# Attention units regrouped by batch in eight phases, mask factors copied instead of computed, and two banks for the first keys' results

## The chip, the cores and the metric

The kernel runs on one core of one Trainium2 chip. The metric is the device time of one execution in microseconds (us); lower is better. The kernel before takes 308.17 us, the median of three runs (307.17 to 308.41).

## The reference

Attention with a sliding window of 128 keys and a linear distance bias, followed by a two-layer MLP with the gate h * cos(h). There are 8 batches, 8 heads, 576 positions and 64 columns per head; the MLP sees 4608 tokens of 512 columns and has 2048 hidden columns.

```python
scores = scale * np.matmul(q, k.transpose(0, 1, 3, 2))
slopes = 2.0 ** (-8.0 * (np.arange(H, dtype=np.float32) + 1) / H)
bias = slopes[:, None, None] * (-np.abs(rel).astype(np.float32))[None, :, :]
mask = (rel >= 0) & (rel < window)
scores = np.where(mask, scores + bias[None], -1000000000.0)
scores = scores - np.max(scores, axis=-1, keepdims=True)
attn = np.exp(scores)
attn = attn / (np.sum(attn, axis=-1, keepdims=True) + 1e-09)
...
x = np.ascontiguousarray(attn_out.transpose(0, 2, 1, 3)).reshape(B * S, H * D)
h = x @ w_in
g = h * np.cos(h)
return (g @ w_out).astype(np.float32)
```

## The kernel before

**Units.** Attention is cut into 64 units, eight for each batch, named (batch, block, half): 128 queries by four heads, mostly. Batches 0 and 1 use blocks that begin at multiples of 128; their first and last units hold all eight heads (the last one 64 queries), and the others four. Batches 2 to 7 use *offset* units: blocks of 128 queries that begin 64 later, and the first 64 queries of the batch are computed along with the two units of block 0 ("first keys", lines 817 to 820). A unit goes through score matmuls on TensorE (PE) (L701, or L661 and L675 for offset units), an exponential on ScalarE (ACT) (L757, L735, L748), a multiplication with mask factors on VectorE (DVE) (L794, or L773, L775 and L780), context matmuls with the values (L841 and L843, L829 and L833, or L813 and L815; L819 for first keys), and a division by the row sums on DVE (L885 and L887; L896 and L898 for first keys). The result is transposed into xT, either by DMA (L962, L965, issued by SyncE, SP) or by PE with a copy behind it (L920, L939).

**The MLP** works on nine chunks of 512 tokens. The first layer of a chunk is 64 matmuls of 512 columns (L978), with cos on ACT (L983) and the gate on DVE (L987); the second layer is 64 matmuls as well (L1031), sixteen for each of four tiles of 128 tokens, with a copy (L1038, L1039) and a store (L1043).

**Phases.** The loop over chunks c (L1144) makes one phase each: the first layer of chunk c, then attention units that later chunks need, then the second layer of chunk c. Seven units of batch 0 run ahead of chunk 0. `QUOTA` has how many units a phase takes, `GROUPS` how they are cut; the units of one group share one block of score matmuls. A group of four is a *side* group, whose scores lie side by side in six banks (`home`, L629) and whose exponentials cover two units each. `SLOT` has the banks of other groups, `SIDE` those of the context results of a group of four, `SIDE_KEY` those of the first keys' results.

**The order** is a planner's. Every operation has an occupancy, a latency, a priority (smaller goes first) and the tiles it reads and writes (`op`); `schedule` (L95) lists them greedily by these costs, and each engine then runs its own list in order, with semaphores for what crosses engines. So a change in groups or costs moves instructions on all engines. Scores have priority 2, context 1, the first layer 5 and the second layer 6: on PE the layers fill what attention leaves.

**Loads.** POOL's queue issues the loads of weights, queries, keys and values. For offset batches SP issues the transposes of queries and keys (L447, L450), and three copies of the values shifted by 64 rows (L424, L426, L428) into the space of the first query or key rows (named qrows or krows); the context matmuls of offset units read values and shifted copy. Of a phase's units, the first four (two in phase 0) are always transposed by DMA; the others by DMA if their tokens belong to a chunk after the next, otherwise by PE (L1097 to L1108).

**Mask factors.** Units of batches 0 and 1 multiply with a table `EM`, the exponential of the biases. Offset units use three tables of their own, `own_em` (in the buffer qfirst), `out_em` (in the buffer bias) and `key_em` (in the buffer kfirst), that `band_factors` (L504) makes during phase 0: distances by POOL, window by DVE, 24 exponentials by ACT.

Of the kernel before, what the change touches and what calls it, by code (L numbers as in the profile page):

```python
# [6 lines left out]
ALU = mybir.AluOpType  # L7
ACTF = mybir.ActivationFunctionType
# [279 lines left out]
def bass_alibi_sliding__then__act_gcu_kernel(  # L288
# [8 lines left out]
    with ExitStack() as ctx:  # L297
# [37 lines left out]

        bdif, boff = sb("bdif", [128, 384], F32), sb("boff", [128, 384], F32)


        own_em = qF["q"][:, :, :].rearrange("p a b -> p (a b)").bitcast(BF16).rearrange(
# [11 lines left out]

        GROUPS = [[2] * 4, [4, 3, 1]] + [[4, 4]] * 4 + [[4, 3, 2]]
        SLOT = [4, 6, 2]

        SIDE, SIDE_KEY = [2, 5, 4, 7], [3, 3, 6, 6]

        FIRST, FIRST_PV = [0, 1, 2, 0, 1, 0, 1], [0, 0, 2, 2, 3, 2, 3]
        QUOTA = [8, 8, 8, 8, 8, 8, 9]
        BIASED = [(0, 0, 0)] + [(0, qb, hh) for qb in range(1, 4) for hh in range(2)][:5]
# [144 lines left out]
        def band_factors():  # L504
            op("pool", lambda e: e.iota(bdif[:, 64:192], pattern=[[192, 2], [-1, 64]], base=-192,
                                        channel_multiplier=1,
                                        allow_small_or_imprecise_dtypes=True),
               w=["bdif"], occ=400, lat=480)
            op("pool", lambda e: e.iota(bdif[:, 192:256], pattern=[[-1, 64]], base=-64,
                                        channel_multiplier=1,  # L510
                                        allow_small_or_imprecise_dtypes=True),
               w=["bdif"], occ=300, lat=380)
            op("pool", lambda e: e.iota(bdif[:, 256:384], pattern=[[-1, 128]], base=-64,
                                        channel_multiplier=1,
                                        allow_small_or_imprecise_dtypes=True),
               w=["bdif"], occ=400, lat=480)
            op("dve", lambda e: e.memset(bdif[:, 0:64], -1.0e6), w=["bdif"], occ=100, pri=7)
            op("dve", lambda e: e.memset(bdif[0:64, 192:256], -1.0e6), w=["bdif"], occ=100, pri=7)
            for edge, test in [(-127.0, ALU.is_lt), (0.0, ALU.is_gt)]:
                op("dve", lambda e, edge=edge, test=test: e.tensor_scalar(  # L520
                    boff[:, :], bdif[:, :], edge, -1.0e6, test, ALU.mult),
                   r=["bdif"], w=["boff"], occ=300, lat=380, pri=7)
                op("dve", lambda e: e.tensor_tensor(bdif[:, :], bdif[:, :], boff[:, :], ALU.add),
                   r=["boff"], w=["bdif"], occ=450, lat=530, pri=7)
            for h in range(H):
                g = band_head(h)
                for o, lo, hi, w in [
                        (own_em[:, g, :], 256, 384, [("qF", "q")]),
                        (out_em[0][:, g, :], 64, 192, [("BT", i) for i in range(0, H, 2)]),
                        (key_em[:, g, :], 192, 256, [("qF", "k")])]:  # L530
                    op("act", lambda e, o=o, lo=lo, hi=hi, s=slopes[h]: e.activation(
                        o, bdif[:, lo:hi], ACTF.Exp, scale=s),
                       r=["bdif"], w=w + ["bem"], occ=180 + (hi - lo) * 5 // 7,
                       lat=280 + (hi - lo) * 5 // 7, table=2, pri=7)
            op("dve", lambda e: e.memset(out_em[1][:, :, 0:64], 0.0),
               w=[("BT", i) for i in range(1, H, 2)] + ["bem"], occ=300, pri=7)
            op("dve", lambda e: e.tensor_copy(out_em[1][:, :, 64:128],
                                              out_em[0][:, :, 64:128]),
               w=["bem"], occ=330, lat=410, pri=7)
# [509 lines left out]
        def attention(us, phase):  # L1049
# [4 lines left out]
            for many in sizes:  # L1054
# [89 lines left out]
        for c in range(NCH):  # L1144
# [64 lines left out]
```

## Time and profile before

| | |
|---|---|
| median of three runs | 308.17 us (307.17, 308.17, 308.41) |
| the profiled execution's own time | 307.02 us |
| its span in the trace | 305.2 us |
| PE, DVE, ACT, POOL busy | 97%, 66%, 65%, 32% of the span |
| granted PE clock | 1.00 |
| first layer of chunk 1, first matmul | at 53.92 us |
| second layer of chunks 1 to 6, first matmul | at 67.73, 100.68, 132.58, 164.95, 195.82 and 227.20 us |
| last matmul of the second layer | ends near 302.8 us |

Times in the trace count from the start of the span. Matmuls are pipelined and their ends are modelled, so the distance of two starts tells more than a length; a few per cent of the matmul records are missing. A line number is that of the kernel before.

### The profile page before, as it was taken

To read this page: it belongs to the slowest core of one execution; us is meant where nothing else is said; L and a number is where in the kernel's file an instruction comes from. 1 tells how busy PE (TensorE), PEld (TensorE's weight loads), DVE (VectorE), ACT (ScalarE), POOL (GpSimd) and SP (SyncE) were. 2 spreads that over 40 slices of the span, in tenths; PEclk is the share of its full clock that TensorE was granted. 3 is DMA by queue.
4 is the path that set the end of the run, shared out by engine and by line. 5 is a ranking of instruction groups with operands and counts; after the bars stand their busy time and mean duration, and the time that the engine had idled before them with its cause. 6 is when DMAs were issued, how large, how long until landed. Compare 5 with 4: busy or idle time off the path is not lost.

```text
span 305.2 us, 7209 instructions
## 1 busy us (share of the span) xinstructions
PE 296.6 (97%) x2900; PEld 156.8 (51%) x2945; DVE 200.3 (66%) x482; ACT 198.0 (65%) x292; POOL 96.9 (32%) x124
## 2 busy tenths in 40 slices
PE   8999999999999999999999999999999999999996
PEld 6585455445554455445544554455445554444444
DVE  6687867585778568848686768766984778844000
ACT  6887889985378817882687467846777368854211
POOL 8997200555057304470357006620500000000000
PEclk9999999999999999999999999999999999999999
DMA  8999999999499936999799939997996320001122
GB/s 146 178 207 206 207 163 172 165 212 207 81 133 184 229 70 95 130 181 248 94 171 190 212 65 144 152 167 192 150 109 198 95 74 5 2 0 69 71 76 96
DMA packets 151408, 42.32 MB, mean 139 GB/s; under 512 B 138832, under 2 KB 145616, under 8 KB 151376
## 3 DMA queue, kind: packets, MB, share of 16 engines
q0 software_dynamic: 100416, 18.10, 79.8%
q1 hardware_dynamic: 50688, 23.51, 36.4%
q8 instruction: 23, 0.38, 0.5%
q10 hardware_dynamic: 272, 0.26, 0.3%
q14 instruction: 9, 0.07, 0.1%
HBM read 36.70 MB, written 9.44 MB: 151 GB/s over the span
## 4 chain that ended last, share of the span: by engine, by line
PE 86%; DMA 7%; POOL 4%; issue 2%; ACT 0%; POOLq 0%; ACTq 0%
PE ps L1031 40%; PE ps L978 36%; DMA w_outb<-in_moe_w_out_dram 7%; PE ps L661 2%; PE ps L813 2%; PE ps L815 2%; POOL vp L412 1%; PE ps L675 1%; POOL w_inb L459 1%; PE ps L701 1%; POOL qrows L405 1%; POOL krows L405 1%; PE ps L819 0%; PE ps L939 0%; POOL w_outb L466 0%
## 5 line engine op out<-in xcount | busy, mean ns | idle before, releaser
L1031 PE MATMUL ps<-w_outb,gT 128*128 128x512 bf16 (+2 forms) x564 | 130.3, 373 | 2.9 <-issue 2.1
L978 PE MATMUL ps<-xT,w_inb 128*128 128x512 bf16 x529 | 119.7, 379 | 0.8 <-issue 0.2
L983 ACT ACTIVATE cos<-ps,halfpi 128x512 f32<-128x512 f32 x136 | 89.7, 689 | 23.5 <-PE ps L978 17.7
L987 DVE TENSOR_TENSOR gT<-ps,cos 128x512 bf16<-128x512 f32 x136 | 90.2, 688 | 20.8 <-ACT cos L983 16.0
L1031 PEld LDWEIGHTS ps<-w_outb,gT 128*128 128x128 bf16 x592 | 53.8, 98 | 56.6 <-DMA w_outb<-in_moe_w_out_dram 1.1
L978 PEld LDWEIGHTS ps<-xT,w_inb 128*128 128x128 bf16 x544 | 51.5, 98 | 59.9 <-DVE gT L987 1.0
L412 POOL DMA_DIRECT2D vp<-in_v_dram x40 | 33.7, 868 | 92.3 <-DMA xT<-xnat 71.3
L1038 ACT ACTIVATE ob<-ps 128x512 f32<-128x512 f32 (+2 forms) x24 | 13.9, 579 | 46.3 <-PE ps L1031 30.3
L735 ACT ACTIVATE p<-ps 128x768 bf16<-128x768 f32 x40 | 31.3, 809 | 13.9 <-PE ps L675 13.3
L438 POOL DMA_DIRECT2D qnat<-in_q_dram x30 | 25.3, 877 | 17.5 <-DMA qt<-qnat 17.5
L438 POOL DMA_DIRECT2D knat<-in_k_dram x30 | 25.3, 873 | 10.3 <-DMA kt<-knat 7.6
L1039 DVE COPY ob<-ps 128x512 f32<-128x512 f32 x13 | 9.0, 692 | 27.2 <-PE ps L1031 27.2
L887 DVE TENSOR_TENSOR xnat<-ps,rec 128x256 bf16<-128x256 f32 x60 | 24.9, 419 | 0.6
L773 DVE TENSOR_TENSOR p<-p,qfirst 128x512 bf16<-128x512 bf16 x48 | 19.0, 414 | 8.1 <-ACT p L735 4.9
L757 ACT ACTIVATE p<-ps 128x1024 bf16<-128x1024 f32 x16 | 15.8, 1027 | 7.8 <-PE ps L675 4.0
L775 DVE TENSOR_TENSOR p<-p,bias 128x512 bf16<-128x512 bf16 x48 | 19.0, 411 | 0.2
L813 PEld LDWEIGHTS ps<-vp,p 128*128 128x128 bf16 x192 | 14.8, 97 | 7.2 <-issue 2.7
L813 PE MATMUL ps<-vp,p 128*128 128x65 bf16 x192 | 18.0, 193 | 0.1
L885 DVE RECIPROCAL rec<-ps 128x4 f32<-128x4 f32 x60 | 10.2, 176 | 8.3 <-PE ps L815 5.1
L661 PE MATMUL ps<-qt,kt 64*64 64x128 bf16 x384 | 10.2, 220 | 0.0
L661 PEld LDWEIGHTS ps<-qt,kt 64*64 64x64 bf16 x384 | 7.7, 108 | 4.9 <-issue 3.0
L748 ACT ACTIVATE p<-ps 128x768 bf16<-128x768 f32 x8 | 6.0, 810 | 5.8 <-PE ps L675 5.8
(105 smaller groups left out, 232.4 us busy)
## 6 DMA issues: line engine op xcount, KB each, us to landing
out_dram<-ob SPq DMA_DIRECT2D x35, 256.0 KB, 5.3
vp<-in_v_dram POOLq DMA_DIRECT2D x32, 128.0 KB, 6.4
qnat<-in_q_dram POOLq DMA_DIRECT2D x24, 128.0 KB
knat<-in_k_dram POOLq DMA_DIRECT2D x24, 128.0 KB, 6.9
w_outb<-in_moe_w_out_dram POOLq DMA_DIRECT2D x4, 512.0 KB, 21.9
w_inb<-in_moe_w_in_dram POOLq DMA_DIRECT2D x3, 512.0 KB, 11.5
qrows<-vp SPq DMA_DIRECT2D x3, 264.0 KB, 5.2
krows<-vp SPq DMA_DIRECT2D x3, 264.0 KB, 5.0
```

What stands on the lines that cost most here:

```text
L412: op("pool", [lambda e, t=t, rows=rows: e.dma_start(vp[b % 2][0:rows, t, :, 0:64], v[b, :, 128 * t:128 * t + rows, :].rearrange("h p d -> ...
L438: fns.append(lambda e, t=t, rows=rows: e.dma_start(nat[which][0:rows, t, :, :], src[b, :, 128 * t:128 * t + rows, :].rearrange("h p d -> p ...
L661: ins = e.matmul(flat[64 * half:64 * half + 64, c0:c0 + 128], kt[lo, j, pr, 64 * half:64 * half + 64], two, start=True, stop=True)
L735: op("act", lambda e, x=x, c0=c0: e.activation(p_all[:, i:i + 2, 384 * x:384 * x + 384], flat[:, c0:c0 + 768].rearrange("p (u f) -> p u f" ...
L773: op("dve", lambda e: e.tensor_tensor(p1, p1, own_em[:, gs, :], ALU.mult), r=[("P", i), "bem"], w=[("P", i)], occ=330, lat=420, pri=1)
L775: op("dve", lambda e: e.tensor_tensor(o, p2[:, :, None, :].broadcast_to([128, 4, 2, 64]), out_em[0 if qb else 1][:, gs, :].rearrange("p g ...
L813: e.matmul(o, P[i][:, c0:c0 + 128], V[:, qb, h, 0:65], start=True, stop=False)
L887: op("dve", lambda e: e.tensor_tensor(o, U[:, :, :, 0:64], rv[:, :, :, None].broadcast_to([128, 2, 2, 64]), ALU.mult), r=[("rec", n % 4)], ...
L978: op("pe", lambda e, kc=kc: e.matmul(ps[:, bank, :], w_in[:, kc, 128 * fc:128 * fc + 128], xT[:, kc, r0:r0 + CH], start=(kc == 0), stop=(k ...
L983: op("act", lambda e: e.activation(cosb[ci][:, :], ps[:, bank, :], ACTF.Sin, bias=halfpi[:, 0:1]), r=["halfpi"], w=[("B", bank), ("cos", c ...
L987: op("dve", lambda e: e.tensor_tensor(gT[gi][:, fc, :], ps[:, bank, :], cosb[ci][:, :], ALU.mult), r=[("cos", ci)], w=[("B", bank)] + [("g ...
L1031: op("pe", lambda e, t=t, fc=fc, bank=bank, j0=j0, j1=j1: e.matmul(ps[:, bank, 0:j1 - j0], gT[gi][:, fc, 128 * t:128 * t + 128], w_out[:, ...
```

## The change

1. The units of phase 0 are nine (one, then four pairs), so that all of batch 1 is done there; phases 1 to 6 take the eight units of one offset batch each, in two groups of four. The exchange that put the last unit of batch 1 among the second group of phase 1 is gone.
2. In a group of four, the results of the first keys go to bank 3 for half 0 and to bank 6 for half 1; before, it was by the place in the group.
3. `band_factors` copies `own_em` and `out_em` out of `EM` (six copies on ACT or DVE), fills the upper half of `key_em` with zeros and copies its lower half out of `own_em`. The three POOL operations, six DVE operations and 24 exponentials go, and the two buffers bdif and boff with them.
4. The loads of the next values and queries ask for one unit more than before (`>` for `>=`), which is the same phase as before, since a phase now ends one unit later.

```diff
-        bdif, boff = sb("bdif", [128, 384], F32), sb("boff", [128, 384], F32)
-        GROUPS = [[2] * 4, [4, 3, 1]] + [[4, 4]] * 4 + [[4, 3, 2]]
+        GROUPS = [[1] + [2] * 4] + [[4, 4]] * 6
-        SIDE, SIDE_KEY = [2, 5, 4, 7], [3, 3, 6, 6]
+        SIDE, SIDE_KEY = [2, 5, 4, 7], [3, 6]
-        QUOTA = [8, 8, 8, 8, 8, 8, 9]
+        QUOTA = [9, 8, 8, 8, 8, 8, 8]
...
         def band_factors():
-            op("pool", lambda e: e.iota(bdif[:, 64:192], pattern=[[192, 2], [-1, 64]], base=-192,
-                                        channel_multiplier=1,
-                                        allow_small_or_imprecise_dtypes=True),
-               w=["bdif"], occ=400, lat=480)
...
-            for h in range(H):
-                g = band_head(h)
-                for o, lo, hi, w in [
-                        (own_em[:, g, :], 256, 384, [("qF", "q")]),
-                        (out_em[0][:, g, :], 64, 192, [("BT", i) for i in range(0, H, 2)]),
-                        (key_em[:, g, :], 192, 256, [("qF", "k")])]:
-                    op("act", lambda e, o=o, lo=lo, hi=hi, s=slopes[h]: e.activation(
-                        o, bdif[:, lo:hi], ACTF.Exp, scale=s),
-                       r=["bdif"], w=w + ["bem"], occ=180 + (hi - lo) * 5 // 7,
-                       lat=280 + (hi - lo) * 5 // 7, table=2, pri=7)
+            for hh in range(2):
+                gs, ks = slice(4 * hh, 4 * hh + 4), slice(2 * hh, 2 * hh + 2)
+                for o, c0, n, w in [(own_em[:, gs, 0:64], 192, 64, [("qF", "q")]),
+                                    (own_em[:, gs, 64:128], 0, 64, [("qF", "q")]),
+                                    (out_em[0][:, gs, :], 64, 128,
+                                     [("BT", i) for i in range(0, H, 2)])]:
+                    o = o.rearrange("p (x k) f -> p x k f", x=2)
+                    i_ = EM[:, :, ks, c0:c0 + n]
+                    op(("act", "dve"),
+                       {"act": lambda e, o=o, i_=i_: e.activation(o, i_, ACTF.Copy),
+                        "dve": lambda e, o=o, i_=i_: e.tensor_copy(o, i_)},
+                       r=[("EM", 0), ("EM", 1), ("tr", "q", 1, 0)], w=w + ["bem"],
+                       occ={"act": 70 + 5 * n, "dve": 60 + 5 * n},
+                       lat={"act": 170 + 5 * n, "dve": 140 + 5 * n}, pri=7)
...
+            op("dve", lambda e: e.memset(key_em[0:64, :, :], 0.0), w=[("qF", "k"), "bem"],
+               occ=200, pri=7)
+            op("dve", lambda e: e.tensor_copy(key_em[64:128, :, :], own_em[64:128, :, 0:64]),
                w=["bem"], occ=330, lat=410, pri=7)
...
-                        kbank[u] = SIDE_KEY[n] if side else SLOT[n] + 1
+                        kbank[u] = SIDE_KEY[u[2]] if side else SLOT[n] + 1
...
         every = [u for b in range(B) for u in units(b)]
-        every.insert(19, every.pop(15))
...
-            while next_v < B and done >= 8 * (next_v - 1):
+            while next_v < B and done > 8 * (next_v - 1):
...
-            while next_t < B and done >= 8 * (next_t - 1):
+            while next_t < B and done > 8 * (next_t - 1):
```

Three places show what this does to the order on PE; the line numbers of the changed kernel are 11 smaller behind `band_factors`. The first is the start of phase 0, the first score block after chunk 0's first layer. Before (x is a count; 128x64 scores are those of batch 0's last unit, 128x128 those of batch 1):

```order
L978 MATMUL ps<-xT,w_inb 128x512 x7
L1031 MATMUL ps<-w_outb,gT0 128x512 x10
L701 MATMUL ps<-qt0,kt0 128x64 x16
L701 MATMUL ps<-qt1,kt1 128x128 x8
L1031 MATMUL ps<-w_outb,gT0 128x512 x14
```

And in the changed kernel:

```order
L967 MATMUL ps<-xT,w_inb 128x512 x7
L1020 MATMUL ps<-w_outb,gT0 128x512 x4
L690 MATMUL ps<-qt0,kt0 128x64 x16
L1020 MATMUL ps<-w_outb,gT0 128x512 x13
L690 MATMUL ps<-qt1,kt1 128x128 x16
```

The last unit of batch 0 has a block of its own, six second-layer matmuls earlier, and thirteen second-layer matmuls follow instead of fourteen. At the end of phase 0, the changed kernel leaves six of the 64 second-layer matmuls of chunk 0 for after chunk 1's first layer; before, none.

The second place is the end of phase 1. Before, behind the context matmuls of the second group (xtail1 is the last unit of batch 1):

```order
L1031 MATMUL ps<-w_outb,gT1 128x512 x2
L920 MATMUL ps<-ident,xtail1 128x64 x4
L1031 MATMUL ps<-w_outb,gT1 128x512
L939 MATMUL ps<-ident,xnat4 128x128 x2
L1031 MATMUL ps<-w_outb,gT1 128x512
L939 MATMUL ps<-ident,xnat5 128x128 x2
L661 MATMUL ps<-qt0,kt0 64x128 x8
L675 MATMUL ps<-qt0,kt0 64x64 x8
L978 MATMUL ps<-xT,w_inb 128x512 x9
```

And in the changed kernel:

```order
L928 MATMUL ps<-ident,xnat4 128x128 x2
L1020 MATMUL ps<-w_outb,gT1 128x512 x3
L928 MATMUL ps<-ident,xnat5 128x128 x2
L967 MATMUL ps<-xT,w_inb 128x512 x2
L802 MATMUL ps<-vp0,p 128x65
```

The transposes of the tail unit are gone (SP issues a DMA for it, behind the copies of batch 2's values), and so is the third score block, of a single unit. In the whole program PE has 40 transposes of results before and 32 after, and 18 and 17 blocks of scores in phases 0 to 6.

The third place is the first context block of phase 3, behind the last scores of its first group. Before (vp1 and krows are batch 3's values and shifted copy, vp0 and qrows batch 4's):

```order
L661 MATMUL ps<-qt0,kt0 64x128 x8
L675 MATMUL ps<-qt0,kt0 64x64 x8
L1031 MATMUL ps<-w_outb,gT1 128x512 x21
L813 MATMUL ps<-vp1,p 128x65
L815 MATMUL ps<-krows,p 128x65
```

And in the changed kernel:

```order
L650 MATMUL ps<-qt0,kt0 64x128 x8
L664 MATMUL ps<-qt0,kt0 64x64 x8
L1020 MATMUL ps<-w_outb,gT1 128x512 x21
L802 MATMUL ps<-vp0,p 128x65
L804 MATMUL ps<-qrows,p 128x65
```

The block stands 21 second-layer matmuls behind the scores in both, but it is batch 3's last unit before and batch 4's first unit after.

More of the change, by code (lines that the diff above doesn't have):

```diff
@@ L504, in band_factors @@
         def band_factors():
-            op("pool", lambda e: e.iota(bdif[:, 64:192], pattern=[[192, 2], [-1, 64]], base=-192,
-                                        channel_multiplier=1,
-                                        allow_small_or_imprecise_dtypes=True),
-               w=["bdif"], occ=400, lat=480)
[L509 to L524, printed above, removed]
@@ L538, in band_factors @@
                                               out_em[0][:, :, 64:128]),
+               w=["bem"], occ=330, lat=410, pri=7)
+            op("dve", lambda e: e.memset(key_em[0:64, :, :], 0.0), w=[("qF", "k"), "bem"],
+               occ=200, pri=7)
+            op("dve", lambda e: e.tensor_copy(key_em[64:128, :, :], own_em[64:128, :, 0:64]),
                w=["bem"], occ=330, lat=410, pri=7)
```

## The prediction, as it stands on record

> **What bounds the kernel now.** I read the page first, then TensorE's timeline, then the busy time by stages. The page gives the busy time of each engine and the shares of the chain that ended last.
>
> ```profile
> PE 296.6 (97%) x2900; PEld 156.8 (51%) x2945; DVE 200.3 (66%) x482; ACT 198.0 (65%) x292; POOL 96.9 (32%) x124
> ```
> ```profile
> PE 86%; DMA 7%; POOL 4%; issue 2%; ACT 0%; POOLq 0%; ACTq 0%
> ```
>
> TensorE ends the chain, but "97% busy" alone proves little, since a matmul's modelled length overlaps the next one's. The timeline settles it; its columns are start, length, engine, line, names and count. This is phase 1, in three pieces.
>
> ```profile
> 67.73 1.89 PE L1031 MATMUL ps<-w_outb,gT 128*128 128x512 bf16 x8
> 69.57 0.31 PE L661 MATMUL ps<-qt,kt 64*64 64x128 bf16 x8
> ...
> 70.62 4.48 PE L1031 MATMUL ps<-w_outb,gT 128*128 128x512 bf16 x20 [0.16 <-issue]
> 74.94 0.19 PE L813 MATMUL ps<-vp,p 128*128 128x65 bf16 x1
> ...
> 84.81 0.59 PE L1031 MATMUL ps<-w_outb,gT 128*128 128x512 bf16 x2
> 85.33 0.29 PE L920 MATMUL ps<-ident,xtail 64*128 64x64 bf16 x4
> 85.78 0.28 PE L939 MATMUL ps<-ident,xnat 128*128 128x128 bf16 x2 [0.16 <-issue]
> 85.89 0.38 PE L1031 MATMUL ps<-w_outb,gT 128*128 128x512 bf16 x1
> 86.11 0.28 PE L939 MATMUL ps<-ident,xnat 128*128 128x128 bf16 x2
> 86.31 0.31 PE L661 MATMUL ps<-qt,kt 64*64 64x128 bf16 x8
> ...
> 86.62 2.11 PE L978 MATMUL ps<-xT,w_inb 128*128 128x512 bf16 x9
> ```
>
> Twenty matmuls start within 4.48 - 0.38 = 4.10 us: 19 steps of 0.216 us. What follows a stream starts as its last step ends, so TensorE is not waiting here; each instruction taken from its queue shortens the run by its step. The Trainium skill's page "TensorE: Matmul & The Clock Gate", section "Back-to-back issue gap", gives about 131 ns as the sustained step of a 512-column matmul in a stream with weight loads. The trace disagrees, with 216 ns. By the page's figure some 40% of TensorE's time would be slack and the sum below would be zero.
>
> The stages agree that little waiting is left. In the table by stages, phase 2 and phase 3 (first column: from, to, length) do the same work and differ by 0.47 us; the timeline has a hole in the middle of a score block of phase 3, with no cause but "issue".
>
> ```profile
> 100.68:132.58 31.90, 31.37 (x325) 16.09 (x330) 23.07 (x57) 20.81 (x29) 9.45 (x12) 1.00 1.29 125
> 132.58:164.95 32.37, 31.62 (x326) 16.18 (x330) 23.07 (x57) 20.81 (x29) 15.60 (x19) 1.00 1.62 178
> ```
> ```profile
> 145.93 0.22 PE L675 MATMUL ps<-qt,kt 64*64 64x64 bf16 x3 [0.27 <-issue]
> ```
>
> **The change, step by step.** All sums stand against the profiled execution's own 307.02 us: 305.2 of span and 1.8 around it. That is 1.15 us under the median of 308.17; the prediction is put on the median's scale by adding that.
>
> *Transposes taken from TensorE: -0.54 us.* The tail unit of batch 1 moves from phase 1 to phase 0, where its tokens belong to a later chunk, so its four transposes (L920) become a DMA. From 85.33 to 85.89 stand, by the program's order, these four, one second-layer matmul (0.22, its record is missing) and one pair of transposes (0.11, from 85.78 to 85.89): 0.56 - 0.22 - 0.11 = 0.23. The two matmuls from 84.81 need 0.43 and the block starts 0.52 later, so switching costs 0.09 more: 0.32 in all. One pair each in phases 2 and 3 goes too, since the unit now stands among the first four and is transposed by DMA: 2 x 0.11 = 0.22. The DMA that takes its place stands last of five on SP and has the 18 second-layer matmuls and the score block of the second four to land in (18 x 0.216 + 0.95 = 4.8 us).
>
> *Score blocks: -0.22 us.* The units are the same 64, but phases 0, 1 and 6 had 4, 3 and 3 blocks and get 5, 2 and 2: 18 become 17. The cost of a block's edges follows from two sizes. A block of four: 69.57 less 8 x 0.216 from 67.73 leaves 0.11 ahead; from 69.57 to 74.94 are 5.37 us with 21 second-layer matmuls (4.53) in the order, so 0.84; together 0.95. A block of one: 86.31 to 86.62 is 0.31, with 86.11 + 0.11 to 86.31 ahead, 0.09: 0.40. The difference is 0.18 a unit, and 0.22 is left per block.
>
> *First waits for the second layer's weights: +0.28 us.* They come in four quarters, and each output tile needs all four.
>
> ```profile
> 34.07 2.63 PE L1031 MATMUL ps<-w_outb,gT 128*128 128x512 bf16 x10
> 36.63 0.63 PE L701 MATMUL ps<-qt,kt 64*128 64x64 bf16 x24
> 37.19 3.35 PE L1031 MATMUL ps<-w_outb,gT 128*128 128x512 bf16 x13
> ...
> 42.38 0.41 PE L829 MATMUL ps<-vp,p 128*128 128x65 bf16 x8
> ...
> 53.92 13.97 PE L978 MATMUL ps<-xT,w_inb 128*128 128x512 bf16 x63
> ```
> ```profile
> 15.05 20.99 DMA w_outb<-in_moe_w_out_dram
> ```
> ```profile
> 14.30 2.99 POOL L466 DMA_DIRECT2D w_outb<-in_moe_w_out_dram  x4
> ```
> ```profile
> DMA to landing us min/median/max: 21.0/21.9/22.8
> ```
>
> The second quarter lands at 15.05 + 20.99 = 36.04; the third is issued at 14.30 + 2 x 0.75 = 15.8 and takes the longest time in the last row (second and third quarter): 38.6. Two output banks take eight matmuls for each quarter. Before, the ninth waits from 34.07 + 8 x 0.216 = 35.80 to 36.04, and the seventeenth from 37.19 + 6 x 0.216 = 38.49 to 38.6: 0.35 together. After, four matmuls, a small score block (about 0.44 with its edge: the 0.56 from 36.63 to 37.19 less its eight wide matmuls, 0.22, plus 0.10 ahead) and thirteen matmuls stand in a row, and the seventeenth comes at 34.07 + 16 x 0.216 + 0.44 = 37.97: it waits 0.63, in order, and score block and context matmuls of the next units wait behind it. The loads on POOL's queue ahead of it are the same, so their landing is too.
>
> *Phase 0 has nine units: nothing, 0 to +0.9.* The extra work is moved, not added. But TensorE now reaches chunk 1's first layer earlier: six second-layer matmuls are put off into phase 1 (-1.30), a unit and an edge of scores more (0.18 + 0.22), one pair of transposes less (-0.11), the wait (+0.28): 53.92 - 0.73 = 53.2. What it needs there is the first unit of batch 1, transposed by DMA:
>
> ```profile
> 45.24 1.30 SPq L962 DMA_TRANSPOSE xT<-xfirst  x1
> ```
> ```profile
> xT<-xfirst SPq DMA_TRANSPOSE x1, 8.4
> ```
> ```profile
> 64.07 1.25 SPq L450 DMA_TRANSPOSE kt<-knat  x1
> ```
> ```profile
> DMA to landing us min/median/max: 5.0/5.0/5.0
> ```
>
> It lands at 45.24 + 8.4 = 53.6. The unit's context matmuls keep their time (42.4), but VectorE and SP have one mask and one store less ahead of the transpose, and I put it a microsecond earlier: 52.6, no wait. If it lands as before, 0.4 is lost, and 0.6 if also the weights' wait shrinks. Then the last key transpose of batch 2, landed at 64.07 + 5.0 = 69.1, is met by the first score block at 69.57 - 0.73 + 0.6 = 69.4: 0 to 0.3.
>
> *Copies in place of 24 exponentials: nothing, -0.1 to +0.5.*
>
> ```profile
> L537 DVE COPY bias<-bias 128x512 bf16<-128x512 bf16 x1 | 0.6, 550 | 0.0
> ```
> ```profile
> 38.35 0.69 DVE L794 TENSOR_TENSOR p<-p,emask 128x1024 bf16<-128x1024 bf16 x1 [0.74 <-ACT p L757]
> ```
>
> ScalarE loses 24 exponentials and gets two copies; it has 0% of the chain, so that is worth nothing. VectorE loses six operations, four of them over 384 f32 columns, and gets six, the widest of them like the row of 512 bf16 columns with 0.55 us: as an estimate, no more than 6 x 0.55 = 3.3 us come and, by the width, about half as much goes, all ahead of phase 0's first mask. That mask had 0.74 us of idle time ahead of it, and the weights' wait of 0.63 stands before its context block: 3.3 - 1.65 - 0.74 - 0.63 leaves 0.3 at the worst. If that cover were gone, it would cost 0.5 or so.
>
> *The first context block of phases 2 to 6: nothing, 0 to +1.3.* It now belongs to the new batch, so it waits for the copy of that batch's shifted values, which before only the second block did; behind it on TensorE's queue stand the phase's whole second layer and the next scores.
>
> ```profile
> 133.16 0.89 SPq L428 DMA_DIRECT2D qrows<-vp  x1
> ```
> ```profile
> DMA to landing us min/median/max: 6.0/6.0/6.0
> ```
> ```profile
> 139.79 0.19 PE L813 MATMUL ps<-vp,p 128*128 128x65 bf16 x1
> ```
> ```profile
> 196.30 0.92 SPq L428 DMA_DIRECT2D qrows<-vp  x1
> ```
>
> In phase 3 the copy lands at 139.2, 0.6 ahead of the block. In phase 5 it lands at 196.30 + 6.0 = 202.3, and the block stands at about 203.2 by the same 5.37 us after its score block: 0.9 ahead. Nothing new stands ahead of the copies on SP, so I take zero; one more SP slot of 1.25 us would cost 0.65 + 0.35, rounded up to 1.3 with the same slot lost to a DMA transpose of the phase's own units in phases 2 and 3.
>
> Sum: -0.54 - 0.22 + 0.28 = **-0.48**: 306.54 of its own, **307.7** on the median's scale.
>
> **The rivals.**
> *The copies of the values come late (slower).* If loads and transposes shift so that the copy lands s later, phases 3 and 5 lose s - 0.6 and s - 0.9. The gain is gone from s = 1.0 (0.4 + 0.1); half a per cent is lost from s = 1.75; two slots of SP, 2.5 us, cost 1.9 + 1.6 = 3.5, and the time is 307.7 + 3.5 = 311.2. For it: margins under a microsecond, DMA engines near full. Against it: the chain begins at the first unit's transpose, and that keeps its place.
> *Phase 0 and 1 become fed by DMA.* All bounds of that part come true: 0.6 + 0.3 + 0.5, so 309.1. For it: the transpose already lands 0.3 before its use.
> *The holes close.* The weights' wait of 0.35 goes instead of growing, and the hole of 0.47 in phase 3 is chance: -0.76 - 0.35 - 0.47 = -1.58, so 306.6. For it: an "issue" hole has no cause in the trace. Against it: the third quarter lands when it lands.
> *TensorE is not the bound.* Then nothing shows: 308.2. The 0.216 us step speaks against it.
>
> **How the numbers follow.** Forecast 0.50, late copies 0.18, DMA-fed start 0.15, closed holes 0.13, no effect 0.04. A measurement of this kernel tells about 0.5%, 1.5 us, from no change. Faster by more: the closed holes, 0.13. Slower by more: the late copies and the upper end of the DMA-fed start with them, 0.18 + 0.03 = 0.21. Within: 0.50 + 0.12 + 0.04 = 0.66. The range runs from 306.2, under the closed holes, to 310.6, late copies with s near 2.2.
>
> **What would show it.** Right: no L920 record on xtail, 28 transposes of pairs, 17 score blocks, a wait of about 0.6 us on the second layer near 38 us, and stages of phases 2 to 6 that differ by no more than 0.5 us from their counts. Wrong: TensorE idle ahead of L978 near 53 us, or ahead of a phase's first context block, released by a DMA; or phase stretches longer at equal counts, which would mean VectorE feeds TensorE too late.

## The result, and the profile after

The changed kernel takes 305.94 us (median of eight runs, 305.23 to 308.51), the kernel before beside it 307.56 us (eight runs, 307.17 to 309.41). The ratio is 0.9945, with a 95% interval of 0.9922 to 0.9968: about 1.7 us faster. Three later sets, described below, gave 0.9937, 0.9927 and 0.9934. The forecast was 307.7 us in a range from 306.2, so the gain is three to four times the forecast 0.48, and in the direction of the rival "the holes close" (306.6). Part of the distance to 307.7 is scale: the forecast stands on the median of three runs of the kernel before, 308.17, which is 0.6 us above that of the eight runs beside the change. The first profiled execution after took 305.70 us (span 303.9), that of before 307.02 us.

The page of the changed kernel has these shares of engines and of the chain. Records that were missing before are all there after, so PE's busy time is not to be compared:

```profile
PE 299.2 (98%) x2937; PEld 157.0 (52%) x2937; DVE 196.9 (65%) x478; ACT 194.4 (64%) x271; POOL 96.3 (32%) x121
```
```profile
PE 94%; DMA 3%; POOL 2%; issue 0%; ACT 0%; POOLq 0%; ACTq 0%
```

The end of phase 1 in the changed kernel's timeline of TensorE, without the context matmuls:

```profile
70.50 4.71 PE L1020 MATMUL ps<-w_outb,gT 128*128 128x512 bf16 x21
...
86.30 0.27 PE L928 MATMUL ps<-ident,xnat 128*128 128x128 bf16 x2
86.41 0.81 PE L1020 MATMUL ps<-w_outb,gT 128*128 128x512 bf16 x3
87.05 0.28 PE L928 MATMUL ps<-ident,xnat 128*128 128x128 bf16 x2
87.17 0.59 PE L967 MATMUL ps<-xT,w_inb 128*128 128x512 bf16 x2
```

The transposes of the tail unit and the third score block are gone. A pair of transposes costs 86.41 - 86.30 = 0.11 us, as priced. In the busy time by stages, phases 2 and 3 read:

```profile
101.22:132.70 31.48, 31.48 (x328) 16.03 (x327) 21.82 (x55) 20.74 (x29) 9.69 (x12) 1.00 1.34 139
132.70:164.74 32.04, 32.04 (x330) 16.12 (x329) 22.60 (x57) 20.55 (x29) 12.59 (x15) 1.00 1.62 163
```

Phase 3 has two second-layer matmuls more (0.43 us), so 31.91 would be its length without waits; another 0.13 is waiting.

**Five traces of each.** One pair of traces differs by 1.3 us, but a single trace holds waits that come and go. So both kernels were traced four times more. The table has the mean of five, and in brackets the shortest, of the distances between fixed points of TensorE's order. The first row is the time at which the third quarter of the second layer's weights has landed; the chunk's seventeenth second-layer matmul needs it.

| from the row above to | before | after |
|---|---|---|
| third quarter of w_out landed | 38.60 | 38.51 |
| first context block of batch 1 | 3.99 (3.79) | 3.82 (3.79) |
| second layer of chunk 1 | 25.43 (25.35) | 25.27 (25.27) |
| second layer of chunk 2 | 33.33 (32.94) | 33.38 (33.38) |
| second layer of chunk 3 | 31.90 (31.90) | 31.48 (31.48) |
| second layer of chunk 4 | 31.99 (31.90) | 32.66 (32.04) |
| second layer of chunk 5 | 30.89 (30.86) | 31.48 (31.48) |
| second layer of chunk 6 | 31.64 (31.38) | 31.90 (31.89) |
| last matmul | 75.32 (75.32) | 73.12 (73.12) |

The means add up to a difference of 1.47 us. The shortest add up to 263.44 and 262.45; phase 3 took 31.92 in the experiment with idle exponentials below, whose order there is the same, so 262.33, and **1.1 us is fixed**, that is, left when each stretch is taken at its shortest. The rest is 0.1 from the landing and 0.3 from waits that before had more of: 1.05 us against 0.78. Their places differ:

```profile
PE ps L661 <- DMA kt<-knat: 1.3, 1, 1.3
```
```profile
PE ps L813 <- DMA qrows<-vp: 0.8, 1, 0.8
```
```profile
PE ps L802 <- DMA qrows<-vp: 1.2, 1, 1.2
```

(Waits in the fifth and the third trace of the kernel before, and in the second trace of the changed kernel: what waited for which DMA, in all, times, the longest.) Before, the first score block of phase 1 waits for the last key transpose of batch 2, in one trace phase 5 for the copied values; the changed kernel waits in phase 3 for the copied values.

### The profile page after: what moved, and what is told of

It is laid out like the page before. It is cut to its first block, busy times and chain, and to the rows that moved or that the text cites. A ratio compares the mean times of both kernels' runs of the same rounds, so it can differ in the third digit from the quotient of the medians.

```text
span 303.9 us, 7193 instructions
## 1 busy us (share of the span) xinstructions
PE 299.2 (98%) x2937; PEld 157.0 (52%) x2937; DVE 196.9 (65%) x478; ACT 194.4 (64%) x271; POOL 96.3 (32%) x121
## 4 chain that ended last, share of the span: by engine, by line
PE 94%; DMA 3%; POOL 2%; issue 0%; ACT 0%; POOLq 0%; ACTq 0%
PE ps L1020 41%; PE ps L967 39%; DMA vp<-in_v_dram 3%; PE ps L991 2%; PE ps L650 2%; PE ps L802 2%; PE ps L804 2%; PE ps L690 1%; PE ps L664 1%; PE ps L572 1%; POOL vp L410 1%; PE ps L928 1%; POOL qrows L403 1%; PE ps L808 1%; POOL krows L403 0%; PE ps L830 0%
## 5 line engine op out<-in xcount | busy, mean ns | idle before, releaser
L1020 PE MATMUL ps<-w_outb,gT 128*128 128x512 bf16 (+2 forms) x592 | 133.8, 373 | 0.0
L967 PE MATMUL ps<-xT,w_inb 128*128 128x512 bf16 x544 | 122.8, 379 | 0.0
L1028 DVE COPY ob<-ps 128x512 f32<-128x512 f32 x12 | 8.2, 687 | 17.3 <-PE ps L1020 17.3
L664 PE MATMUL ps<-qt,kt 64*64 64x64 bf16 x384 | 9.2, 191 | 0.0
```

Source lines behind the costliest of these rows:

```text
L967: op("pe", lambda e, kc=kc: e.matmul(ps[:, bank, :], w_in[:, kc, 128 * fc:128 * fc + 128], xT[:, kc, r0:r0 + CH], start=(kc == 0), stop=(k ...
L1020: op("pe", lambda e, t=t, fc=fc, bank=bank, j0=j0, j1=j1: e.matmul(ps[:, bank, 0:j1 - j0], gT[gi][:, fc, 128 * t:128 * t + 128], w_out[:, ...
```

## Experiments

Line numbers are each kernel's own. The kernels of one set ran on the same chip.

**The changed kernel again** (four times; the last three of these labels stand with later sets).

> The changed kernel once more, for a second trace. Theory A (fixed steps: TensorE simply has fewer instructions and fewer block edges): the time is again about 1.6 us under the kernel before, and the stretch from the start of chunk 0's second layer to the end of the run is 269.0 us within 0.3. Theory B (chance waits and holes that fell in before's profiled run): that stretch moves by 0.5 us or more from one trace to the next. The late values near 15 us (0.89 us of waiting in the first trace): by chance, so 0 to 0.9 here; if TensorE starts chunk 0's second layer near 34.1 us instead of 34.9, the wait for the third quarter of the second layer's weights, absent in the first trace, should show with about 0.6 us.

> The changed kernel a third time, beside the others of this set: 306.1 us. Theory E (phase 0 is fed by the loads until batch 1's first values are there): the first context block of batch 1 starts within 0.5 us of the landing of its value tile (near 42.2 us), however late chunk 0's second layer begins, and the waits ahead of it (late values near 15 us, weights near 36 us) are paid out of the same slack. Rival: a later start of the second layer moves everything behind it by as much.

> The changed kernel, traced a fourth time: 306.1 us; phase 3's first context block waits for the copied values (1.33 and 0.86 us in two of three traces so far), the other phases have none of 0.3 us or more.

> The changed kernel beside it: 306.0 us; its trace has the wait of phase 3 in some size between 0 and 1.4 us, phase 1 takes 33.4 us, phases 2, 4 and 5 take 31.5, 31.5 and 31.9 us, and the first block of batch 1's values starts 0.25 to 0.45 us after they land.

Measured: 306.1 us (ratio 0.9937, 0.9915 to 0.996), 305.95 (0.9927, 0.9901 to 0.9952), one traced execution at 305.66, and 305.68 (0.9934, 0.991 to 0.9958). The wait for the third quarter is there whenever the second layer begins early. The second trace of the changed kernel, and below it the first:

```profile
33.85 1.03 PE L1020 MATMUL ps<-w_outb,gT 128*128 128x512 bf16 x4
34.81 0.41 PE L690 MATMUL ps<-qt,kt 64*128 64x64 bf16 x16
35.15 0.39 PE L1020 MATMUL ps<-w_outb,gT 128*128 128x512 bf16 x1
35.88 2.97 PE L1020 MATMUL ps<-w_outb,gT 128*128 128x512 bf16 x12 [0.34 <-DMA w_outb<-in_moe_w_out_dram]
38.78 0.62 PE L690 MATMUL ps<-qt,kt 64*128 64x128 bf16 x16
...
42.21 0.42 PE L818 MATMUL ps<-vp,p 128*128 128x65 bf16 x8
```
```profile
15.59 0.20 PE L830 MATMUL ps<-vp,p 128*128 128x65 bf16 x1 [0.89 <-DMA vp<-in_v_dram]
...
34.93 1.03 PE L1020 MATMUL ps<-w_outb,gT 128*128 128x512 bf16 x4
35.89 0.41 PE L690 MATMUL ps<-qt,kt 64*128 64x64 bf16 x16
36.23 2.98 PE L1020 MATMUL ps<-w_outb,gT 128*128 128x512 bf16 x13
...
42.57 0.41 PE L818 MATMUL ps<-vp,p 128*128 128x65 bf16 x8
```

Twelve matmuls from 35.88 should take 2.59 us, and the next block comes at 38.78, 2.90 later with 0.11 of switching: 0.2 more, at the third quarter. With the 0.51 from 35.15 to 35.88 above a step, at the second quarter, that makes 0.7 us of waiting. In the first trace, values that came late had cost 0.89 us at 15.59, the second layer began 1.08 us later and did not wait; at the first context block of batch 1 (42.21 and 42.57) only 0.36 of the 1.08 is left. From the second layer's start to the end of the span the second trace has 304.8 - 33.85 = 270.95 us, 2 us more than the first: theory B is right that this stretch moves. Theory E holds with a correction: it is the weights' landing rather than the values' that sets this point, 3.79 or 3.80 us after it in four of the five traces after (3.91 in the first), and 3.79 in three of five before. What TensorE loses earlier is not paid.

**The kernel before again** (timed once more, and three single executions with a trace).

> The kernel before once more, for a second trace and a null comparison (ratio 1.000). The stretch from the start of chunk 0's second layer to the end was 271.1 us. Theory A: the 0.47 us hole in phase 3's score block is gone, but what phases 1, 5 and 6 spent beyond the changed kernel (0.61, 0.35 and 0.45 us) is there again, at the same places: 270.6 us. Theory B: phases 5 and 6 lose no more than their score blocks, holes stand elsewhere or nowhere: 270.0 us or less.

> The kernel before, traced again. If its typical execution (307.8 us) loses 0.8 us more than the traced ones in chance waits: a wait for a DMA of 0.4 us or more in phases 1 to 6 that the earlier traces do not have. If not: the same waits as before (0.17 us twice in phase 5, the weights in phase 0) and 307.1 us.

> As the first of these looks; of three, a wait that belongs to the grouping should stand at the same place each time, a chance wait at different ones.

> As the first of these looks: a fixed wait stands at the same place in all three, a chance wait at different places; 307.1 to 307.8 us.

Measured: 308.14 us (ratio 1.0006, 0.9982 to 1.003), and single executions of 308.51, 306.57 and 308.46. The 0.47 us hole in phase 3's score block never came back: chance. In the second trace a wait of 0.45 us for key transposes in phase 1 has taken its place, and the stretch to the end is 305.5 - 34.28 = 271.2 us again, more than either theory had. So theory B is right that waits move; theory A is right that phases 5 and 6 are as long as before, 31.38 and 75.32 us to the last matmul. Two waits in phase 5 are in all five traces. TensorE and VectorE there, in the second trace of the kernel before:

```profile
198.83 4.71 PE L1031 MATMUL ps<-w_outb,gT 128*128 128x512 bf16 x21
203.54 0.19 PE L813 MATMUL ps<-vp,p 128*128 128x65 bf16 x1
```
```profile
201.70 0.69 DVE L1039 COPY ob<-ps 128x512 f32<-128x512 f32 x1 [3.84 <-PE ps L1031]
202.31 0.75 DVE L773 TENSOR_TENSOR p<-p,qfirst 128x512 bf16<-128x512 bf16 x2
202.97 0.75 DVE L775 TENSOR_TENSOR p<-p,bias 128x512 bf16<-128x512 bf16 x2
```

And both at the same place in the second trace of the changed kernel:

```profile
200.18 4.71 PE L1020 MATMUL ps<-w_outb,gT 128*128 128x512 bf16 x21
204.72 0.19 PE L802 MATMUL ps<-vp,p 128*128 128x65 bf16 x1
```
```profile
201.97 0.69 DVE L1028 COPY ob<-ps 128x512 f32<-128x512 f32 x1 [2.84 <-PE ps L1020]
202.58 0.75 DVE L762 TENSOR_TENSOR p<-p,qfirst 128x512 bf16<-128x512 bf16 x2
203.25 0.42 DVE L764 TENSOR_TENSOR p<-p,bias 128x512 bf16<-128x512 bf16 x1
```

The 21 matmuls look alike, yet the context block follows 4.71 us after their start before and 4.54 after. 21 steps of 0.216 are 4.53, so before waits 0.17 us, although no idle time is printed: the modelled length of the last matmul (0.38) covers it. The masks stand behind a copy of an output tile on VectorE in both kernels. Before, that copy starts 201.70 - 198.83 = 2.87 us after the 21 matmuls, and the mask that the block needs ends at about 202.97 + 0.42 = 203.39, just ahead of the block. The profile names no releaser there, but in all ten cases of the five traces the block starts 0.15 us after the end of a mask. After, the tile is full earlier, the copy starts at 1.79 us, and the masks are done a microsecond before they are used. It happens twice in phase 5 before (0.33 us).

**One part alone.** In the first, the new groups, quotas and banks stand with the old `band_factors`; in the second, the new `band_factors` with everything else as before.

> New grouping, quotas and banks, with the old band factors (24 exponentials on ScalarE from index tables). Theory A: as the changed kernel, 1.6 us under the kernel before (within 0.4). Theory C (the relief of ScalarE and VectorE in phase 0 pays): half of the gain or more is missing, 0.8 us under it or less, and TensorE waits in phase 0 ahead of context blocks.

> The kernel before with only the copied factors. Theory A: no change (within 0.4 us of the kernel before), TensorE's blocks of phase 0 at the same places. Theory C: 0.8 us or more under it.

Measured: 307.4 us (0.9985, 0.9961 to 1.0009) and 308.12 us (1.000, 0.9977 to 1.0022). **Neither part brings what both bring together.** The copies alone do nothing, as forecast; the grouping alone is worth about 0.5 us by the ratio, with an interval that takes in no change, and the copies make 1.9 of it.

**The exponentials' time on ScalarE.** The first kernel is the changed one with 24 exponentials that nothing reads; the second is the grouping alone with the old exponentials at a higher priority.

```diff
+            for h in range(H):
+                for n in (128, 128, 64):
+                    op("act", lambda e, n=n, s=slopes[h]: e.activation(
+                        scr[:, 0:n], dif[:, 1, 0:n], ACTF.Exp, scale=s),
+                       r=["dif", ("tr", "q", 1, 0)], w=["scr"], occ=180 + n * 5 // 7,
+                       lat=280 + n * 5 // 7, table=2, pri=7)
```
```diff
-                       lat=280 + (hi - lo) * 5 // 7, table=2, pri=7)
+                       lat=280 + (hi - lo) * 5 // 7, table=2, pri=2)
```

> The changed kernel with 24 exponentials of the old sizes and old priority added on ScalarE, which write a scratch tile that nothing reads. Theory D (the copies pay because the old exponentials hold ScalarE's table until after chunk 1's first layer has begun, and the second-layer matmuls put in that gap are missing as cover in phase 1): about 307.3 us, like the grouping alone; the table load near 57 us instead of 55, the first layer of chunk 1 broken after 16 matmuls, and 0.5 to 0.8 us of TensorE's waits at the transposes near 87 us. Rival (the 1.3 us between the grouping alone and the full change are chance, or come from VectorE's or POOL's part of the old factors): 306.1 us.

> The new grouping with the old band factors, whose 24 exponentials get priority 2 instead of 7 and so run ahead of the table load's time. Its first layer of chunk 1 is unbroken. Theory D with the break alone as the cost: 306.1 us, like the full change. Theory D with phase 1's missing cover as the cost (here too fewer second-layer matmuls stand among phase 1's transposes): 306.8 us. If ScalarE's added work costs wherever it stands: 307.3 us.

Measured: 307.07 us (0.9967, 0.9944 to 0.999) and 307.36 us (0.9965, 0.9939 to 0.9992), about 1 us above the changed kernel by the ratios. It was not in this set, and the intervals of single sets just overlap, so the reading rests on the traces. ScalarE and TensorE in the first of them, then its phase 1 by stages:

```profile
54.41 1.56 ACT L523 ACTIVATE scr<-dif 128x128 bf16<-128x128 f32 x5
55.98 1.28 ACT L979 ACT_TABLE_LOAD   x1
```
```profile
55.14 3.62 PE L974 MATMUL ps<-xT,w_inb 128*128 128x512 bf16 x15
58.59 0.81 PE L1027 MATMUL ps<-w_outb,gT 128*128 128x512 bf16 x3
59.24 8.80 PE L974 MATMUL ps<-xT,w_inb 128*128 128x512 bf16 x39
...
86.25 0.59 PE L1027 MATMUL ps<-w_outb,gT 128*128 128x512 bf16 x2
86.87 0.28 PE L935 MATMUL ps<-ident,xnat 128*128 128x128 bf16 x2
...
87.61 0.28 PE L935 MATMUL ps<-ident,xnat 128*128 128x128 bf16 x2
87.95 0.81 PE L974 MATMUL ps<-xT,w_inb 128*128 128x512 bf16 x3
```
```profile
67.87:102.01 34.14, 33.35 (x334) 16.71 (x338) 23.05 (x56) 22.17 (x32) 14.99 (x18) 1.00 1.54 151
```

The exponentials fill ScalarE's gaps until the last moment, and the table for cos is loaded behind them (55.98; 57.03 in the grouping alone, 54.79 and 55.15 in the changed kernel). The planner sees the first layer of chunk 1 run out of banks and puts three second-layer matmuls into it. In its order the cover at the end of phase 1 is then missing: between the two pairs of transposes the changed kernel has three second-layer matmuls (86.41 above), this one only a context block. TensorE waits there: 0.19 ahead of 86.87, and 87.95 - 86.87 = 1.08 for work of 0.46 (two pairs, one block of 0.24). Phase 1 takes 34.14 us instead of 33.38 with one second-layer matmul fewer: 0.97 us lost. The second kernel's first layer is not broken, and its phase 1 loses as much:

```profile
68.47:102.28 33.81, 33.12 (x333) 16.65 (x337) 23.05 (x56) 22.16 (x32) 15.06 (x18) 1.00 1.56 155
```

That is 0.43 longer with two matmuls fewer: 0.86. The grouping alone loses there too: its phase 1 takes 34.00 us with three matmuls fewer, 1.27 lost, 0.46 of it for key transposes. So theory D fits in the version with the missing cover. The times alone don't decide it: 307.36 is nearer to the 307.3 that was said for a cost wherever the exponentials stand, and no run put the cover back. The break of the first layer is not needed for the loss, and neither is VectorE's and POOL's part of the old factors, absent in the first kernel. Both kernels also wait 0.7 us for batch 1's values near 42 us, but the first reaches chunk 1's second layer no later for it (67.87 us with one matmul more done, 67.35 to 67.84 in the five traces after). That the key transposes of batch 2 land later with the exponentials (69.8 to 71.2 us, against 67.3 to 67.9 in the five traces after) adds 0 to 0.5 us; why, was not tried, and in the experiment with more score blocks below they land at 71.0 without them.

**The banks of the first keys' results**, by place in the group again:

```diff
-        SIDE, SIDE_KEY = [2, 5, 4, 7], [3, 6]
+        SIDE, SIDE_KEY = [2, 5, 4, 7], [3, 3, 6, 6]
-                        kbank[u] = SIDE_KEY[u[2]] if side else SLOT[n] + 1
+                        kbank[u] = SIDE_KEY[n] if side else SLOT[n] + 1
```

> The changed kernel with the first keys' results of both halves in one bank, by place in the group as before. If the second bank matters, the second unit's first keys wait for VectorE to empty the bank: 0.2 us in each of six phases, 307.3 us. If the second-layer matmuls that are put between cover it: no change, 306.1 us.

Measured: 308.18 us (1.0012, 0.999 to 1.0034): 2.2 us lost, more than either theory said. Its waits on TensorE (by the starts, there are also 0.15 to 0.49 us ahead of the first context block in each of phases 2 to 6):

```profile
PE ps L967 <- DMA xT<-xtail: 1.0, 2, 0.8
PE ps L967 <- ACT p L724: 0.3, 1, 0.3
```

The second unit's first keys are put off by eight second-layer matmuls, so their transpose (xtail) comes late on SP, and the first layer of the next chunk waits. Before, in phases 2 to 6, the two units stood at places 1 and 2 of their group (counted from 0) and had two banks as well; in phase 1 they stood at 0 and 1 and shared one. So the second edit is hardly a gain by itself: it keeps the regrouping from losing.

**The prices of the steps.** The tail unit on TensorE again; and four score blocks more.

```diff
-                        elif late:
+                        elif late and u != (1, 4, 0):
```
```diff
-        GROUPS = [[1] + [2] * 4] + [[4, 4]] * 6
+        GROUPS = [[1] + [2] * 4, [4, 4]] + [[4, 3, 1]] * 4 + [[4, 4]]
```

> The changed kernel with the tail unit of batch 1 transposed on TensorE again (four transposes) instead of by DMA, to measure the largest term of the prediction (0.32 of the 0.54 us): the four transposes and the steps around them cost 0.32 us if the prediction's sizing holds, 0.23 if switching costs nothing there, about 0 if they lie in a gap.

> The changed kernel with phases 2 to 5 in groups of 4, 3 and 1 in place of 4 and 4: four score blocks more, nothing else. By the prediction's price of a block's edges (0.22 us) the four phases grow by 0.88 us together: 307.0 us. If what phases 1 and 6 lost with their third block is the price (0.3 to 0.45 us each, waits of short groups included): 1.2 to 1.8 us, 307.3 to 307.9.

Phase 0 of the first, and of the changed kernel's first trace, neither with a wait for weights:

```profile
35.34:68.57 33.23, 32.76 (x310) 17.14 (x314) 25.10 (x60) 24.12 (x35) 8.38 (x10) 1.00 1.86 181
```
```profile
34.93:67.84 32.91, 32.91 (x312) 17.11 (x310) 25.16 (x59) 24.42 (x35) 8.42 (x11) 1.00 1.85 181
```

The difference is 0.32 us, what the prediction said of this step (its one execution took 307.34 us, with waits elsewhere). The second kernel takes 308.25 us (1.0015, 0.9991 to 1.0039), 2.3 us more than the changed one beside it, and above both forecasts. Two of its waits are of the kinds that come and go in the other traces:

```profile
PE ps L650 <- DMA kt<-knat: 1.6, 1, 1.6
...
PE ps L802 <- DMA qrows<-vp: 0.7, 1, 0.7
```

Its trace begins chunk 2's second layer at 102.58 and the last matmul at 304.63, 202.05 us; after's first trace has 301.24 - 101.22 = 200.02, 0.12 of it waiting in phase 3 above 31.92. Of the extra 2.15, 0.85 is the wait for copied values in phase 3 (counted from the starts; the row's 0.7 leaves out what the modelled length covers), so four blocks, with the short waits that they bring, cost 1.3: **0.33 us each, not 0.22.** The wait of 1.6 us for key transposes is in phase 1, ahead of this stretch, where the order is that of the changed kernel. One trace cannot say how much of the median's other 1.0 us belongs to the extra blocks.

**Against the wait for the copied values.** First the loads that the copy waits for were let go earlier; then the copy was cut in two, so that the first blocks do not wait for tiles that they don't read.

```diff
-                load_v(next_v, behind=begin)
+                load_v(next_v, behind=begin[:2])
```
```diff
-               r=[("v", b % 2, t) for t in range(NBLK)] + [("vinit", b % 2)],
+               r=[("v", b % 2, t) for t in range(3)] + [("vinit", b % 2)],
...
+            op("sp", [
+                lambda e: e.dma_start(W[0:64, 2:4, :, :].rearrange("p t h c -> p (t h c)"),
+                                      V[0:64, 3:5, :, :].rearrange("p t h c -> p (t h c)"))],
+               r=[("v", b % 2, t) for t in range(3, NBLK)] + [("vinit", b % 2), ("vb", b % 2)],
+               w=[("vc", b % 2)], dma=f"cw{b % 2}", occ=600, lat=3500, pri=4)
```

> The changed kernel with the next batch's value loads waiting for the first two DMA transposes of the phase instead of all. If the copy of the shifted values is what phase 3's first context block waited for (1.33 us in the second trace of the changed kernel, 0 in the first): no wait there, phase 3 takes 31.9 us, and the time is 0.3 to 0.7 us under the changed kernel's 306.1. Rival (the loads slow the transposes that the next first layer needs): a wait ahead of the first layer near 118 or 150 us, and 306.1 us or more.

> The changed kernel with the copy of the shifted values in two parts: what the first two blocks of a batch read (value tiles 0 to 2) is copied as soon as these tiles have landed, the rest later; TensorE's order is the same. If phase 3's first context block waits for the copy of the last tiles, which it does not read, the wait is gone: phase 3 takes 31.9 us in the trace, and the median falls by 0.3 to 0.6 us under the changed kernel's run of this set. Rival (the copies wait on SP behind the key transposes anyway, or the queue's fourth copy delays the transposes behind it): no change, or 0.3 us worse.

> The changed kernel with the copy of the shifted values in two parts, timed again beside the changed kernel. If the wait in phase 3 (0.5 us in the mean of four traces) is typical of the timed executions and the split has no price: 0.3 to 0.6 us under the changed kernel. If the split's fourth copy or the waits it opens (0.02 to 0.10 us ahead of the third block in each phase) cost as much: the same within 0.3 us. Phase 3 takes 32.0 us in the trace either way.

The early loads cost: 313.84 us (1.0184, 1.0144 to 1.0225). TensorE's waits, and the stages around phase 3's end:

```profile
PE ps L967 <- DMA xT<-xnat: 2.3, 1, 2.3
```
```profile
151.40:156.40 5.00, 1.88 (x20) 1.10 (x18) 2.58 (x9) 3.54 (x5) 3.17 (x4) 0.82 0.58 55
156.40:161.20 4.80, 4.76 (x19) 1.99 (x20) 1.95 (x7) 1.37 (x2) 1.03 (x2) 0.50 1.57 143
```

The rival was right: with the loads let go earlier, the first layer waits for a transpose of the phase's own units. The split copy gave 306.58 us (0.9947, 0.9922 to 0.9971) and 306.45 us (0.9957, 0.993 to 0.9984), no better than the changed kernel beside it (305.95 and 305.68). The wait for the copies is gone in both traces, but in the second one phase 3 takes 33.32 us all the same, and waits for other DMAs' sake:

```profile
PE ps L1026 <- ACT ob L1033: 0.5, 1, 0.5
...
PE ps L973 <- DMA xT<-xnat: 0.2, 1, 0.2
```

(ScalarE's copy in the first row had itself waited for a store of the output.) So with one wait taken away others can stand in the same phase; whether they were uncovered or are chance, two traces cannot say. No version tried beats the changed kernel.

## Why the prediction was wrong, point by point

The path was right and the sum was not. The steps that failed are two of its terms: score blocks and weights together, put at +0.06, and the waits ahead of context blocks, put at nothing. The traces show -0.23 for each. With the transposes, the fixed gain is 1.1 us in place of 0.48; landing and chance waits add 0.4 in the mean of the traces.

To size the terms, all distances between starts on TensorE were added up by kind, from the seventeenth second-layer matmul to the end, in two traces without missing records (the fourth of the kernel before, the fifth of the changed one). Both do 1087 steps of the layers in this stretch.

| kind | before | after | difference | forecast |
|---|---|---|---|---|
| transposes with the switches around them | 1.55 | 0.93 | -0.62 | -0.54 |
| score blocks with their switches | 13.99 | 13.76 | -0.23 | -0.22 + 0.28 |
| waits ahead of context blocks, without the copied values | 0.50 | 0.27 | -0.23 | 0 |

- *That TensorE bounds the kernel, and a step taken from it counts:* right. The table adds up to the 1.1 us that are fixed. (The 131 ns of the Trainium skill's page "TensorE: Matmul & The Clock Gate", section "Back-to-back issue gap", would have made all of this free; the step in both kernels is 216 ns.)
- *Transposes, -0.54:* right, 0.32 of it measured alone.
- *Score blocks, -0.22 for one:* under-sized. A block cost 0.33 where four were added, short waits included. Phase 1's second group cost another 0.09: in it the scores of batch 1's tail unit are followed by those of batch 2, of another tile shape, and in all five traces before the first of these starts 0.12 us after the last of those (80.1 to 82.0 us), where those follow each other within 0.04.
- *The second layer's weights, +0.28:* the wait came (0.7 us in the second trace, most of it at the second quarter; forecast 0.63 at the third), and it is a real term: 0.22 us of score matmuls now stand behind the landing instead of ahead of it, which the score row holds; without it that row would be -0.45. It was set against too small a saving.
- *Masks in phase 5:* the step that was missing. The prediction took the context blocks of before as waiting for nothing, because the timeline shows no idle time there; 0.33 us were hidden under modelled lengths. That the masks are what it waits for is read from the times, not from an experiment. The changed kernel has one such wait of its own, 0.17 in phase 1.
- *Copies in place of exponentials, nothing:* right on the old grouping and **wrong on the new one**. That ScalarE had 0% of the chain said only that its lateness was covered. The prediction looked for what VectorE's copies would hold up and did not ask what the 24 exponentials would hold up once the groups had moved: 0.97 us of phase 1. Neither the kernel before nor the changed one pays this, so it is no part of the miss in the sum. That the grouping alone gave 0.5 by the ratio, just the size of the sum, is luck: a larger saving and a loss that the sum has neither of.
- *Phase 0 fed by DMA:* no loss. Units of batch 1 reach the first layer's transposes in time. The last key transpose of batch 2, put down as 0 to 0.3 of loss, is a wait of before (0 to 1.3, 0.4 in the mean of five) that none of five traces after has; the 1.6 us of the kernel with more blocks show that the new order can meet it too.
- *Late copies of values, the rival on the slower side:* it came true in phase 3, in three of five traces (0.86 to 1.33 us) at the margin of 0.6 that the prediction had read; not in phase 5, where before has it once (0.98). It takes back 0.65 us in the mean, and the change gains in spite of it.
- *The holes close:* the hole in phase 3 was chance, as it said; the weights' wait did not go.

What stays open: the traces' means differ by 1.5 us, the medians of the four timed sets by 1.6 to 2.2. Five traces are too few to say whether the executions without a trace lose more in the chance waits.

## What to carry to other kernels

An engine with no share of the chain is free only in the order that the trace shows: when a change moves work past it, put its freed work back as idle operations and see what that costs. Two edits that each do little alone may need each other, so try each without the other before one is called useless. And where matmul lengths are modelled, look for short waits in the distances between starts, against the step, not in the printed idle time.

## What the runs showed of the hardware

With the early loads, the gap in TensorE's starts ahead of the first layer was 2.50 us (from the end of the last step at 151.65 to 154.15). The granted clock was 1.00 through this gap and until 154.6, half a microsecond after TensorE had begun again; then it was 0.50 until 161.4, 6.8 us long, with matmuls 0.427 us apart instead of 0.216. Phase 3 took 38.20 us against 32.04: of the 6.2 us, 2.5 are the gap and, as an estimate, half of the 6.8 us at the half clock, 3.4, are lost to it. So the wait cost more than twice itself. The Trainium skill's page "TensorE: Matmul & The Clock Gate", section "Part 1: The HAM clock gate", says that an idle window of about 3.4 us halves the clock and that a busy one of that length restores it. The trace agrees that the clock halves after idling and comes back under work; but here a gap of 2.50 us was enough, and the slow stretch was twice 3.4 us. None of the other traces has it (mean granted clock 1.000 in each).
